# Decode attention on one core: K and V loaded as whole heads of 4 MB instead of halves of 2 MB

## The chip, the cores and the metric

The kernel runs on one core of a Trainium2 chip. The metric is the device time of one execution in microseconds (us). The kernel before takes 325.22 us (median; 324.94 to 325.31). The core's engines are named as in the profile: PE (TensorE matmul), PEld (weight load), DVE (VectorE), ACT (ScalarE), SP (SyncE, which issues the loads here). A trace's span, from its first to its last instruction, is about 2 us shorter than this time (322.9 us for the kernel before).

## The reference

One query row attends to 8,192 keys in each of 16 heads; all inputs are bfloat16.

```python
B, H, Sq, Sk, D = 1, 16, 1, 8192, 256      # q (1,16,1,256), k and v (1,16,8192,256)
scale  = D ** -0.5
scores = einsum("bhqd,bhkd->bhqk", q, k) * scale
p      = softmax(scores, axis=-1)
out    = einsum("bhqk,bhkd->bhqd", p, v)
```

K and V are 134.2 MB together and each byte is used once. A head has 4 MB of K and 4 MB of V.

## The kernel before

A head's 8,192 rows are laid over 128 partitions, 64 rows (columns of 256 elements) in each: 32 KB of a partition for a head. K and V come in halves of 32 columns: 2 MB, 16 KB in each partition. There are four slots of 2 MB for K and four for V.

```python
HALF = 32; K_SLOTS = V_SLOTS = 4; LAG = 4      # (cut: constants put on one line)
FIRST_CUT = (4, 4, 8, 16)                      # the first half of K0 in pieces
LAST_CUT, BEFORE_CUT = (16, 8, 4, 4), (16, 16) # the last two halves of V in pieces

kseq = [(h, x) for h in range(H) for x in range(2)]
for n, kx in enumerate(kseq):                  # order of loads: V four halves behind K
    items.append(("k", *kx))
    while nv <= n - LAG:
        items.append(("v", *kseq[nv])); nv += 1

# ... one load: waits until the half of four before it has been used
    if n >= slots:
        waits = [f"{kind}free{n - slots}"] + ([f"ktfree{n - slots}"] if kind == "k" else [])
    plan.op("sp", lambda e, ...: e.dma_start(b[:, at * D : (at + wd) * D], cols(t, h, c + at, c + at + wd)),
            f"{kind}{n}.{i}", waits, dma=(s, used[id(s)]))
```

For each half of K, DVE computes 24 columns of scores (a multiply with a sum, about 0.345 us a column) and PE the other 8 (16 transposes, a copy by ACT, 16 small matmuls). PE then multiplies the weights of an earlier head with its V ("P·V" below, 32 matmuls per half). One pass of PE's loop, a turn, is:

```python
for h in range(H):                  # PE's program, cut to its order
    softmax(h - 1); k_turn(2 * h); softmax2(h - 1); k_score(2 * h); lmm(h - 1)
    pv(2 * (h - 2))                 # first half of V of head h-2
    k_turn(2 * h + 1); k_score(2 * h + 1)
    pv(2 * (h - 2) + 1)             # second half
    final(h - 2)
```

## Time and profile before

A load is shared by 16 DMA engines. A row is the part of a load that goes to one partition, and moves as one packet. A landing record is the time at which one engine has finished its share. Loads are named by tensor and head: V13 (or v13) is V of head 13.

| view | reading |
|---|---|
| queue table | the loads take 98.1% of the span of the 16 DMA engines |
| busy times | DVE 86%, PE 69% of the span |
| packet records of the trace | 16 KB row: 611 ns (8 KB: 309, 4 KB: 159, 2 KB: 84, at the shortest 81), the most frequent value of each |
| landing records, mean of a load's 16 engines | one 2 MB load every 4.89 to 4.90 us |
| landing records, last engine | last piece of V at 319.65 us |
| PE timeline | last matmul ends at 320.86 us |

These are lines of the page of the kernel before: granted clock of PE, busy share of the DMA engines and GB/s, each in 40 equal slices of the span (9 is 90% or more), then the queue of the loads (packets, MB, share of the span) and the first line of the chain that ended last.

```profile
PEclk9999999999698998989595989777989697897799
DMA  7999999999999999999999999999999999999993
GB/s 276 421 436 428 421 430 428 424 426 426 431 428 426 428 428 428 432 426 424 432 426 434 426 424 430 428 428 429 426 430 426 430 427 428 428 426 428 426 417 120
q1 hardware_dynamic: 10224, 134.22, 98.1%
DVE 52%; DMA 37%; PE 5%; issue 5%; DVEq 1%; ACT 0%; SPq 0%
```

The chain names DVE most, because it follows each load back to the compute that freed its slot. The DMA line decides: no slice but the first and the last is below 9.

PE's timeline of the end of the kernel before (line 607 is P·V; the bracket is the idle time before the first instruction and what ended it):

```profile
299.91 8.81 PE L607 MATMUL acc<-Vb,E 128*1 128x256 bf16 x64 [1.33 <-DMA Vb<-in_v_dram]
308.56 0.38 PE L547 MATMUL misc<-ident,m 128*1 128x128 f32 x2
309.74 1.91 PE L607 MATMUL acc<-Vb,E 128*1 128x256 bf16 x16 [0.80 <-DMA Vb<-in_v_dram]
311.58 0.38 PE L558 MATMUL misc<-g,ones_row 1*128 1x1 f32 x2
311.89 1.91 PE L607 MATMUL acc<-Vb,E 128*1 128x256 bf16 x16
313.63 0.19 PE L587 MATMUL misc<-ones_col,lsum 128*1 128x1 f32 x2
313.69 7.17 PE L607 MATMUL acc<-Vb,E 128*1 128x256 bf16 x64
```

From the landing of the second half of V13 (299.87 us) PE has five blocks of 32 left and needs 20.9 us for them. It ends 1.2 us after the last load.

### The profile page before, as it was taken

To read this page: it belongs to the slowest core of one execution; us is meant where nothing else is said; L and a number is where in the kernel's file an instruction comes from. 1 tells how busy PE (TensorE), PEld (TensorE's weight loads), DVE (VectorE), ACT (ScalarE), POOL (GpSimd) and SP (SyncE) were. 2 spreads that over 40 slices of the span, in tenths; PEclk is the share of its full clock that TensorE was granted. 3 is DMA by queue.
4 is the path that set the end of the run, shared out by engine and by line. 5 is a ranking of instruction groups with operands and counts; after the bars stand their busy time and mean duration, and the time that the engine had idled before them with its cause. 6 is when DMAs were issued, how large, how long until landed. Compare 5 with 4: busy or idle time off the path is not lost.

```text
span 322.9 us, 6455 instructions
## 1 busy us (share of the span) xinstructions
PE 222.2 (69%) x2166; PEld 155.6 (48%) x2166; DVE 277.8 (86%) x1607; ACT 94.1 (29%) x185; POOL 0.2 (0%) x4
## 2 busy tenths in 40 slices
PE   1554328766586858686987756886665966668897
PEld 0333225655364635454564534564543644455565
DVE  3799999999999999999998988889988889888600
ACT  3362321432324242323142242212422123232010
POOL 0000000000000000000000000000000000000000
PEclk9999999999698998989595989777989697897799
DMA  7999999999999999999999999999999999999993
GB/s 276 421 436 428 421 430 428 424 426 426 431 428 426 428 428 428 432 426 424 432 426 434 426 424 430 428 428 429 426 430 426 430 427 428 428 426 428 426 417 120
DMA packets 10271, 134.37 MB, mean 416 GB/s; under 512 B 1154, under 2 KB 1171, under 8 KB 1940
## 3 DMA queue, kind: packets, MB, share of 16 engines
q1 hardware_dynamic: 10224, 134.22, 98.1%
q8 instruction: 5, 0.08, 0.1%
q14 instruction: 6, 0.05, 0.0%
q10 hardware_dynamic: 36, 0.02, 0.0%
HBM read 134.23 MB, written 0.01 MB: 416 GB/s over the span
## 4 chain that ended last, share of the span: by engine, by line
DVE 52%; DMA 37%; PE 5%; issue 5%; DVEq 1%; ACT 0%; SPq 0%
DVE prod L360 48%; DMA Kb<-in_k_dram 19%; DMA Vb<-in_v_dram 18%; PE acc L607 5%; DVE S L360 2%; DVE g L332 1%; DVE colf L286 0%; DVE recip L341 0%; DVEq L145 0%; DVE m L379 0%; ACT o L621 0%; DVEq L138 0%; DVEq L139 0%; SPq L319 0%; PE misc L558 0%
## 5 line engine op out<-in xcount | busy, mean ns | idle before, releaser
L360 DVE CUSTOM_DVE_ANT_0 prod<-Kb,qbc 128x256 bf16<-128x256 bf16 x768 | 269.1, 411 | 24.6 <-DMA Kb<-in_k_dram 15.7
L607 PE MATMUL acc<-Vb,E 128*1 128x256 bf16 x1024 | 147.4, 314 | 8.8 <-DMA Vb<-in_v_dram 8.8
L607 PEld LDWEIGHTS acc<-Vb,E 128*1 128x1 bf16 x1024 | 96.3, 96 | 52.4 <-DMA Vb<-in_v_dram 9.9
L502 ACT ACTIVATE KT<-tp 128x1024 bf16<-128x1024 bf16 x64 | 62.0, 1021 | 118.2 <-PE tp L493 118.2
L360 DVE DVE_READ_ACCUMULATOR2_ANT S<- 128x1 f32 x768 | 56.8, 74 | 0.0
L493 PE MATMUL tp<-identb,Kb 128*128 128x128 bf16 x512 | 38.2, 234 | 7.8 <-DMA Kb<-in_k_dram 7.8
L493 PEld LDWEIGHTS tp<-identb,Kb 128*128 128x128 bf16 x512 | 32.3, 105 | 15.7 <-issue 14.2
L519 PE MATMUL spe<-qcur,KT 128*128 128x1 bf16 x512 | 20.6, 165 | 19.7 <-ACT KT L502 19.7
L558 PE MATMUL misc<-g,ones_row 1*128 1x1 f32 x32 | 7.1, 287 | 36.1 <-DVE g L332 36.1
L519 PEld LDWEIGHTS spe<-qcur,KT 128*128 128x128 bf16 x512 | 16.4, 99 | 24.5 <-ACT KT L502 24.3
L621 ACT ACTIVATE o<-acc,recip 1x256 bf16<-1x256 f32 x16 | 7.4, 464 | 69.4 <-PE acc L607 69.4
L558 PEld LDWEIGHTS misc<-g,ones_row 1*128 1x128 f32 x32 | 5.7, 221 | 39.1 <-DVE g L332 38.8
L547 PE MATMUL misc<-ident,m 128*1 128x128 f32 x34 | 7.1, 293 | 18.6 <-DVE m L379 18.6
L547 PEld LDWEIGHTS misc<-ident,m 128*1 128x1 f32 x34 | 1.9, 82 | 22.0 <-DVE m L379 21.4
L565 ACT ACTIVATE negb<-misc 128x1 f32<-128x1 f32 x16 | 2.7, 171 | 27.4 <-PE misc L558 27.4
L332 DVE TENSOR_REDUCE g<-misc 1x1 f32<-1x128 f32 x17 | 4.7, 274 | 5.2 <-PE misc L547 5.2
L341 DVE RECIPROCAL recip<-misc 1x1 f32<-1x1 f32 x17 | 2.6, 151 | 4.6 <-PE misc L587 4.6
L572 ACT ACTIVATE E<-S,negb 128x64 bf16<-128x64 f32 x16 | 5.6, 348 | 0.7 <-ACT negb L565 0.2
L587 PE MATMUL misc<-ones_col,lsum 128*1 128x1 f32 x34 | 3.2, 164 | 3.7 <-ACT E L572 3.7
L439 ACT ACTIVATE qbc<-qb 128x256 bf16<-128x256 bf16 x14 | 5.6, 400 | 0.0
L532 ACT ACTIVATE S<-spe 128x16 f32<-128x16 f32 x16 | 2.9, 183 | 7.2 <-PE spe L519 7.2
L413 PE MATMUL tp<-q,identb 16*128 16x256 bf16 x15 | 4.1, 406 | 0.6 <-ACT qb L422 0.5
(29 smaller groups left out, 22.7 us busy)
## 6 DMA issues: line engine op xcount, KB each, us to landing
Kb<-in_k_dram SPq DMA_DIRECT2D x31, 2048.0 KB, 24.3
Vb<-in_v_dram SPq DMA_DIRECT2D x30, 2048.0 KB, 29.5
Vb<-in_v_dram SPq DMA_DIRECT2D x3, 1024.0 KB, 16.5
Kb<-in_k_dram SPq DMA_DIRECT2D x1, 1024.0 KB, 8.5
Kb<-in_k_dram SPq DMA_DIRECT2D x2, 256.0 KB, 3.0
Kb<-in_k_dram SPq DMA_DIRECT2D x1, 512.0 KB, 6.5
Vb<-in_v_dram SPq DMA_DIRECT2D x1, 512.0 KB, 12.7
Vb<-in_v_dram SPq DMA_DIRECT2D x2, 256.0 KB, 13.0
```

The costliest lines, as they stand in the source:

```text
L332: lambda e: e.tensor_reduce(g[0:1, s : s + 1], misc[s][0:1, MT0 : MT0 + P], AX.X, ALU.max),
L360: lambda e, slot=slot, c=c, col=col, h=h, r=(ttr - 1) % PROD: e.tensor_tensor_reduce(out=prod[:, r * D : (r + 1) * D], in0=Kb[slot][:, c * ...
L413: lambda e, i=i, src=src: e.matmul(bank[:, i * D : (i + 1) * D], lhsT=src[0], rhs=src[1], start=True, stop=True),
L439: lambda e: e.activation(out=qbc[:, s * D : (s + 1) * D], in_=qb[:, (h - 2) * D : (h - 1) * D], func=ACT.Copy),
L493: lambda e, c=c, hf=hf, i=(b * NH + hf) * P, view=view: e.transpose(view[:, i : i + P], Kb[slot][:, c * D + hf * P : c * D + (hf + 1) * P] ...
L502: lambda e, gn=gn, view=view: e.activation(out=KT[gn % KT_SLOTS][:, :], in_=view[:, 0 : GROUP * D], func=ACT.Copy),
L519: lambda e, b=b, hf=hf, oc=oc, gn=gn: e.matmul(spe[sl(h)][:, oc : oc + 1], lhsT=KT[gn % KT_SLOTS][:, (b * NH + hf) * P : (b * NH + hf + 1) ...
L547: lambda e: e.matmul(misc[s][0:1, MT0 : MT0 + P], lhsT=m[:, s : s + 1], rhs=ident[:, :], start=True, stop=True),
L558: lambda e: e.matmul(misc[s][:, BC0 : BC0 + 1], lhsT=ones_row[0:1, :], rhs=g[0:1, s : s + 1], start=True, stop=True),
L572: lambda e: e.activation(out=E[:, s * J : (s + 1) * J], in_=S[:, s * J : (s + 1) * J], func=ACT.Exp, bias=negb[:, h : h + 1], scale=SCALE, ...
L607: lambda e, c=c, col=col: e.matmul(a[0:1, 0:D], lhsT=E[:, col : col + 1], rhs=Vb[slot][:, c * D : (c + 1) * D], start=(x == 0 and c == 0), ...
L621: lambda e: e.activation(out=o[0:1, h * D : (h + 1) * D], in_=acc[s][0:1, 0:D], func=ACT.Copy, scale=recip[0:1, s : s + 1],),
```

## The change

Its intent: fewer and larger transfers, with rows of 32 KB instead of 16 KB, to come nearer to the peak of the DMA engines. K and V get two slots of 4 MB each instead of four of 2 MB; the SBUF used is the same. V runs one head behind K for the first eight heads, then two (before, four halves, which is two heads, throughout). Both halves of P·V move to the end of the turn, since V now lands whole.

```diff
-K_SLOTS = 2 * UNROLL
-V_SLOTS = 2 * UNROLL
-FIRST_CUT = (4, 4, 8, 16)
-LAST_CUT = (16, 8, 4, 4)
-BEFORE_CUT = (16, 16)
-LAG = 4
+K_CUTS = {0: (4, 4, 8, 16, 32)}
+V_CUTS = {14: (32, 16, 16), 15: (16, 16, 16, 8, 4, 4)}
+LAG_FROM = 8
@@ buffers
-        Kb = [sb([P, HALF * D], dt, "Kb") for _ in range(K_SLOTS)]
-        Vb = [sb([P, HALF * D], dt, "Vb") for _ in range(V_SLOTS)]
+        Kb = [sb([P, J * D], dt, "Kb") for _ in range(2)]          # J = 64 columns
+        Vb = [sb([P, J * D], dt, "Vb") for _ in range(2)]
@@ order of loads
+        for h in range(H):
+            loads.append(("k", h))
+            done = sum(kind == "v" for kind, _ in loads)
+            loads += [("v", x) for x in range(done, h + 1 - (1 if h < LAG_FROM else 2))]
@@ what a load waits for
-            if n >= slots:
-                waits = [f"{kind}free{n - slots}"] + ([f"ktfree{n - slots}"] if kind == "k" else [])
+            if h >= 2:
+                waits = [f"{f}{n}" for n in (2 * h - 4, 2 * h - 3) for f in ((kind + "free", "ktfree") if kind == "k" else ("vfree",))]
@@ PE's turn
                 lmm(h - 1)
                 if h + 1 < H:
                     q_row(h + 1)
-                if h >= 2:
-                    pv(2 * (h - 2))
...
             k_turn(2 * h + 1)
             k_score(2 * h + 1)
             if h >= 2:
+                pv(2 * (h - 2))
                 pv(2 * (h - 2) + 1)
                 final(h - 2)
```

More of the change, by code (lines that the diff above doesn't have):

```diff
@@ L213, in bass_standalone__mha_softmax__decode_kernel @@
         sems = {e: sem(f"s_{e}") for e in plan.ops}
-        s_k = [sem(f"s_k{i}") for i in range(K_SLOTS)]
-        s_v = [sem(f"s_v{i}") for i in range(V_SLOTS)]
-        s_first = [sem(f"s_f{i}") for i in range(len(FIRST_CUT) - 1)]
-        s_last = [sem(f"s_l{i}") for i in range(len(LAST_CUT) + len(BEFORE_CUT) - 2)]
+        s_k = [sem(f"s_k{i}") for i in range(2)]
+        s_v = [sem(f"s_v{i}") for i in range(2)]
+        s_piece = {}
         s_q = sem("s_q")
@@ L243, in bass_standalone__mha_softmax__decode_kernel, with cuts, pieces @@
         kseq = [(h, x) for h in range(H) for x in range(2)]
-        NIT = 2 * H
-        items, nv = [], 0
-        for n, kx in enumerate(kseq):
-            items.append(("k", *kx))
-            while nv <= n - LAG:
-                items.append(("v", *kseq[nv]))
-                nv += 1
-        items += [("v", *kx) for kx in kseq[nv:]]
-        n_of = {kx: n for n, kx in enumerate(kseq)}
-        def cuts(kind, n):
-            if kind == "k" and n == 0:
-                return FIRST_CUT
-            if kind == "v" and n == NIT - 1:
-                return LAST_CUT
-            if kind == "v" and n == NIT - 2:
-                return BEFORE_CUT
-            return (HALF,)
-        def landed(kind, n, c0, c1):
-            names, at = [], 0
-            if kind == "k" and n and n % K_SLOTS == 0:
-                names = [f"k{n}.0"] + [x for x in landed(kind, 0, c0, c1) if x != "k0.0"]
-                return names
-            for i, w in enumerate(cuts(kind, n)):
-                if at < c1 and at + w > c0:
-                    names.append(f"{kind}{n}.{i}")
-                at += w
-            return names
+        loads = []
+        for h in range(H):
+            loads.append(("k", h))
+            done = sum(kind == "v" for kind, _ in loads)
+            loads += [("v", x) for x in range(done, h + 1 - (1 if h < LAG_FROM else 2))]
+        loads += [("v", x) for x in range(sum(kind == "v" for kind, _ in loads), H)]
+        def cuts(kind, h):
+            return (K_CUTS if kind == "k" else V_CUTS).get(h, (J,))
+        def landed(kind, n, c0, c1):
+            h, x = kseq[n]
+            def pieces(h):
+                at = 0
+                for i, w in enumerate(cuts(kind, h)):
+                    if at < x * HALF + c1 and at + w > x * HALF + c0:
+                        yield i
+                    at += w
+            if kind == "k" and h and h % 2 == 0:
+                return [f"k{h}.0"] + [f"k0.{i}" for i in pieces(0) if i]
+            return [f"{kind}{h}.{i}" for i in pieces(h)]
         def dve(fn, name=None, waits=(), sem=None):
@@ L301, in bass_standalone__mha_softmax__decode_kernel @@
         plan.op("act", lambda e: e.dma_start(q16[:, :], q[0, :, 0, :]), "q", dma=(s_q, 16))
-        for kind, h, x in items:
-            n = n_of[(h, x)]
-            slots, sem_l, t, buf = (K_SLOTS, s_k, k, Kb) if kind == "k" else (V_SLOTS, s_v, v, Vb)
-            slot = n % slots
+        for kind, h in loads:
+            sem_l, t, buf = (s_k, k, Kb) if kind == "k" else (s_v, v, Vb)
             waits = []
-            if n >= slots:
-                waits = [f"{kind}free{n - slots}"] + ([f"ktfree{n - slots}"] if kind == "k" else [])
-            cs = cuts(kind, n)
+            if h >= 2:
+                waits = [f"{f}{n}" for n in (2 * h - 4, 2 * h - 3) for f in ((kind + "free", "ktfree") if kind == "k" else ("vfree",))]
+            cs = cuts(kind, h)
             at = 0
             for i, wd in enumerate(cs):
-                if kind == "k":
-                    s = sem_l[slot] if i == 0 else s_first[i - 1]
-                else:
-                    s = sem_l[slot] if i == len(cs) - 1 else s_last[i + (len(LAST_CUT) - 1) * (n == NIT - 2)]
+                s = sem_l[h % 2]
+                if i != (0 if kind == "k" else len(cs) - 1):
+                    s = s_piece[(kind, h, i)] = sem(f"s_{kind}{h}_{i}")
                 used[id(s)] = used.get(id(s), 0) + 16
@@ L318, in bass_standalone__mha_softmax__decode_kernel @@
                     "sp",
-                    lambda e, b=buf[slot], t=t, h=h, c=x * HALF, at=at, wd=wd: e.dma_start(
-                        b[:, at * D : (at + wd) * D], cols(t, h, c + at, c + at + wd)
+                    lambda e, b=buf[h % 2], t=t, h=h, at=at, wd=wd: e.dma_start(
+                        b[:, at * D : (at + wd) * D], cols(t, h, at, at + wd)
                     ),
-                    f"{kind}{n}.{i}",
+                    f"{kind}{h}.{i}",
                     waits,
@@ L349, in bass_standalone__mha_softmax__decode_kernel @@
         for n, (h, x) in enumerate(kseq):
-            slot = n % K_SLOTS
             if x == 0 and h % UNROLL == 0:
@@ L359, in bass_standalone__mha_softmax__decode_kernel @@
                 dve(
-                    lambda e, slot=slot, c=c, col=col, h=h, r=(ttr - 1) % PROD: e.tensor_tensor_reduce(
+                    lambda e, c=c, x=x, col=col, h=h, r=(ttr - 1) % PROD: e.tensor_tensor_reduce(
                         out=prod[:, r * D : (r + 1) * D],
-                        in0=Kb[slot][:, c * D : (c + 1) * D],
+                        in0=Kb[h % 2][:, (x * HALF + c) * D : (x * HALF + c + 1) * D],
                         in1=qbc[:, sl(h) * D : (sl(h) + 1) * D],
@@ L480, in k_turn @@
             h, x = kseq[n]
-            slot = n % K_SLOTS
             for gi in range(NG):
@@ L494, in k_turn @@
                                 view[:, i : i + P],
-                                Kb[slot][:, c * D + hf * P : c * D + (hf + 1) * P],
+                                Kb[h % 2][:, (x * HALF + c) * D + hf * P : (x * HALF + c) * D + (hf + 1) * P],
                                 identb[:, :],
@@ L600, in pv @@
             h, x = kseq[n]
-            slot = n % V_SLOTS
             a = acc[sl(h)]
@@ L609, in pv @@
                         lhsT=E[:, col : col + 1],
-                        rhs=Vb[slot][:, c * D : (c + 1) * D],
+                        rhs=Vb[h % 2][:, (x * HALF + c) * D : (x * HALF + c + 1) * D],
                         start=(x == 0 and c == 0),
```

## The prediction

> **What bounds it now.** The loads. The page's slice table shows DMA at 9 in every slice but the first and last, at about 428 GB/s; its queue table gives 98.1% of the 16 engines' span. DVE is busy 86%, PE 69%. In the trace's DMA packet records a 16 KB row takes 611 ns, and a 2 MB load (8 rows per engine, plus a 9 ns completion write) lands 4.90 us after the one before: no gaps. The last V piece lands at 319.65 us; the chain of waits ends with 64 back-to-back matmuls (7.04 us), which end near 320.9. PE and the loads finish almost together.
>
> **What the change does.**
> 1. Rows of 32 KB. Packets of 2, 4, 8 and 16 KB take 81, 159, 309 and 611 ns: about 604 ns per 16 KB plus 7 per packet. My estimate for 32 KB is 1,215 ns, against 1,222 for two. With half the completion writes that saves 0.065 us per 4 MB, over some 30 such loads 2.0 us (0.6%). The Trainium skill ("DMA: Bandwidth & Descriptors", "Why small descriptors are slow") also has a fixed cost per packet; here it is already about 1%, so little is left to take.
> 2. Slots of 4 MB: the same SBUF, freed in coarser steps. From DVE's 17.1 to 17.8 us per head, PE's durations and an estimated 9.73 us per load, K's next load can be issued with several us to spare; V, while it lags by one head (heads 2 to 7), with 0 to 4. v2, at about 64 us, is the tightest early.
> 3. A head's P·V now runs as one block of 64 matmuls at the end of a turn. V13 arrives whole at about 298 us (299.9 in the old order, less the saving). Before, 5 x 32 matmuls remained then; now 6 x 32 do. At 112 ns that is 21.5 us, plus about 0.8 us of softmax steps: 320.3 us at the earliest, later than the loads (about 317.7). The loads' gain is hidden behind PE.
> 4. PE is half idle before that block, so it starts slow. The clock records show 0.5 in windows of 3.41 us after little activity (300.8 to 304.2 us, for instance); P·V blocks of 32 took 3.65 us at full clock and 5.3 with such a window, as the skill says ("TensorE: Matmul & The Clock Gate", Part 1). One window costs about 1.7 us: the last matmul ends near 322.0. V15 also waits for V13's block to end (305 to 308.6 us, needed at about 307.8): a gap of 0 to 2 us in the queue.
>
> **On the critical path:** -2.0 us of packets, +1.5 us for PE's longer tail, +1.7 us of slow clock: about +1 us in sum.
>
> **Predicted: 326.2 us, range 323.6 to 329.0.** Chances: faster by over 2% 0.01, within 2% 0.96, slower by over 2% 0.03.
>
> **Right or wrong shows in:** 32 KB packets of about 1,215 ns and 431 GB/s in middle slices; K landings 19.5 us apart; DMA slices all 9, at most small dents; the last V landing at 317 to 319 us; P·V from V13 on back to back, PE ending 2 to 5 us after the last landing.
>
> **What would make it wrong:** full clock through the tail (then about 324.7); 32 KB rows no faster per byte (+2 us); repeated queue gaps from coarse V slots in heads 2 to 7, over 1 us each (+3 to +8 us); instruction fetches delayed by longer packets.

## More of the kernel before

SP issues the loads in program order: a load whose wait has not ended holds back all that follow.

Why there are no gaps shows in SP's timeline (start us, duration us, engine, line, operation, count), here of a little more than one head.

```profile
97.14 0.33 SPq L319 DMA_DIRECT2D Kb<-in_k_dram  x1
97.54 0.41 SPq L319 DMA_DIRECT2D Vb<-in_v_dram  x1
105.88 0.33 SPq L319 DMA_DIRECT2D Kb<-in_k_dram  x1
107.64 0.33 SPq L319 DMA_DIRECT2D Vb<-in_v_dram  x1
114.25 0.33 SPq L319 DMA_DIRECT2D Kb<-in_k_dram  x1
```

Loads are issued every 5 us on the average, in step with the freeing of halves. The V load issued at 107.64 lands, by the mean of its engines, at 131.43; the load ahead of it lands at 126.53, so it stood in the queue for 18.9 us before that. The queue never runs dry: after the first loads, none is issued less than 4.4 us before the mean landing of the load ahead.

## The result, and the profile after

The changed kernel takes 333.43 us (median of 5; 332.16 to 334.29). Its ratio to the kernel before is 1.0251, with a 95% interval of 1.0229 to 1.0273: slower by 2.5%. Here and below, a ratio is not quite the ratio of the medians that are quoted.

The lines of the page of the changed kernel that answer to those of before:

```profile
PEclk9999999957859588595876959595967878596799
DMA  7999999799998999999999899999999999999883
GB/s 249 438 435 433 426 435 435 283 423 431 433 412 352 435 415 415 443 380 411 431 435 439 332 435 443 439 435 431 411 435 443 439 428 427 423 431 419 344 356 153
q1 hardware_dynamic: 6192, 134.22, 95.8%
DMA 44%; DVE 29%; PE 20%; issue 4%; ACT 2%; SPq 0%; DVEq 0%
```

The rate in the good slices went up, from about 428 GB/s to about 432 (one 4 MB load every 9.71 us; single slices scatter around that). But there are holes: 283, 352, 380 and 332 GB/s in the slices at about 60, 103, 145 and 184 us, and two at the end. The clock line also has more low slices.

The holes, seen closely. Columns: stretch and its length in us; busy us (and instructions) of PE, PEld, DVE, ACT and POOL; PE's clock; DMA's busy share (which can come out a little over 1 in this view); GB/s. First the changed kernel, then the kernel before over the same stretches.

```profile
58.00:66.00 8.00, 6.35 (x65) 4.67 (x63) 5.80 (x35) 0.62 (x2) 0.00 (x0) 1.00 0.72 268
102.00:108.00 6.00, 3.81 (x40) 2.58 (x37) 3.71 (x24) 1.29 (x2) 0.00 (x0) 1.00 0.78 295
184.00:188.00 4.00, 2.99 (x35) 2.22 (x32) 3.97 (x24) 1.88 (x3) 0.00 (x0) 1.00 0.78 262
```

```profile
58.00:66.00 8.00, 5.51 (x66) 4.20 (x66) 7.96 (x48) 3.55 (x6) 0.00 (x0) 1.00 1.00 424
102.00:108.00 6.00, 5.82 (x43) 3.88 (x44) 6.00 (x37) 0.43 (x3) 0.00 (x0) 0.72 1.02 434
184.00:188.00 4.00, 2.93 (x31) 1.99 (x29) 2.81 (x16) 0.46 (x1) 0.00 (x0) 1.00 1.04 442
```

What SP waited for says which releases the loads now hang on (releaser, then us in total, times, longest; a long wait is not yet a hole, as the 185.2 us of the kernel before show). First the kernel before, then the changed one.

```profile
SPq L319 <- DVE S L360: 185.2, 28, 7.7
SPq L319 <- PE acc L607: 61.6, 19, 10.6
```

```profile
SPq L306 <- PE acc L591: 137.4, 11, 19.8
SPq L306 <- DVE S L346: 89.6, 9, 10.8
```

P·V was a minor releaser of loads before (line 607); now it is the main one (line 591), with waits of up to 19.8 us. The landing records of the trace give each late load. The steady spacing of 4 MB loads is 9.71 us, by the mean of the 16 engines' landings; what a load took beyond that is its gap:

| load | issued at | mean landing of the load ahead | issued ahead of it by | gap |
|---|---|---|---|---|
| v2 | 63.21 | 62.81 | -0.40 us | 2.73 us |
| v3 | 83.12 | 85.06 | 1.94 | 0.46 |
| v4 | 104.40 | 104.98 | 0.58 | 1.63 |
| v5 | 124.26 | 126.03 | 1.76 | 0.52 |
| v6 | 144.57 | 145.99 | 1.41 | 0.93 |
| k10 | 185.21 | 185.91 | 0.70 | 1.55 |
| v15, first piece | 314.66 | 313.91 | -0.74 | 2.72 |

The sum of the last two columns is nearly a constant: 2.2 to 2.4 us for the 4 MB loads and 2.0 us for the piece of V15. In these cases a load had to be issued that long before the mean landing of the load ahead of it, or time was lost. In the other runs the same sum is 2.1 to 3.7 us for loads of 2 and 4 MB, the most in front of k9 in the control below. The six gaps ahead of V14 sum to 7.8 us.

The packet records of the trace show what such a gap holds. V4's first packets start 0.95 us after the start of its issue (1.3 us on the mean over the engines); the engines had stood idle for 1.12 us on the mean, and 14 of the 16 first packets then took 1.39 to 2.09 us instead of 1.21, which is 0.57 us more per engine: 1.69 us in sum, against a gap of 1.63. In front of V3 and V5 the engines were idle for only 0.15 us, and most of the gap is slow first packets (0.43 and 0.37 us). Why these are slow is not shown.

One of these turns: SP's timeline, then four lines of PE's (five shorter ones cut; line 478 transposes of K, 591 P·V, 532 the first step of the next softmax).

```profile
104.40 0.33 SPq L306 DMA_DIRECT2D Vb<-in_v_dram  x1
104.77 0.43 SPq L306 DMA_DIRECT2D Kb<-in_k_dram  x1
```

```profile
87.22 1.05 PE L478 MATMUL tp<-identb,Kb 128*128 128x128 bf16 x16 [3.91 <-DMA Kb<-in_k_dram]
92.55 1.89 PE L478 MATMUL tp<-identb,Kb 128*128 128x128 bf16 x16
95.92 8.45 PE L591 MATMUL acc<-Vb,E 128*1 128x256 bf16 x64
104.40 0.38 PE L532 MATMUL misc<-ident,m 128*1 128x128 f32 x2
```

K4 lands on its last engine at 86.98 us and PE's turn starts. The P·V block of V2, whose data had been there since 77.25, starts 8.7 us later and ends at 104.37; only then is the slot of V2 free and V4 issued. But K5, the last load in the queue, has a mean landing of 104.98. V4's data start 1.63 us late, and K6, behind it in SP's order, with it.

At the end, PE's timeline shows the tail:

```profile
304.88 13.24 PE L591 MATMUL acc<-Vb,E 128*1 128x256 bf16 x96 [1.25 <-DMA Vb<-in_v_dram]
317.95 0.38 PE L532 MATMUL misc<-ident,m 128*1 128x128 f32 x2
318.17 1.91 PE L591 MATMUL acc<-Vb,E 128*1 128x256 bf16 x16
320.01 0.38 PE L543 MATMUL misc<-g,ones_row 1*128 1x1 f32 x2
320.32 1.91 PE L591 MATMUL acc<-Vb,E 128*1 128x256 bf16 x16
322.06 0.19 PE L572 MATMUL misc<-ones_col,lsum 128*1 128x1 f32 x2
322.12 7.15 PE L591 MATMUL acc<-Vb,E 128*1 128x256 bf16 x64
```

V13 lands (last engine) at 304.74 us and PE has six blocks of 32 left, which run without a pause to 329.27. The gap of 2.72 us in front of V15 lies in this stretch. It costs nothing further, because PE has not got there yet: the last V lands at 327.01, 2.3 us before the last matmul ends.

So the last matmul ends 8.4 us later than before (320.86). Of that, 5.0 us are the later start of the tail (299.91 to 304.88) and 3.4 us its greater length (20.9 to 24.4 us, for six blocks instead of five).

### The profile page after: what moved, and what is told of

Its sections match the earlier page's. It is cut to its first block, busy times and chain, and to the rows that moved or that the text cites. A ratio compares the mean times of both kernels' runs of the same rounds, so it can differ in the third digit from the quotient of the medians.

```text
span 331.3 us, 6400 instructions
## 1 busy us (share of the span) xinstructions
PE 228.8 (69%) x2166; PEld 166.2 (50%) x2166; DVE 277.4 (84%) x1607; ACT 94.1 (28%) x185; POOL 0.2 (0%) x4
## 4 chain that ended last, share of the span: by engine, by line
DMA 44%; DVE 29%; PE 20%; issue 4%; ACT 2%; SPq 0%; DVEq 0%
DVE prod L346 26%; DMA Kb<-in_k_dram 26%; PE acc L591 18%; DMA Vb<-in_v_dram 18%; ACT KT L487 2%; DVE S L346 1%; PE tp L478 1%; PE misc L543 1%; DVE g L319 0%; ACT E L557 0%; SPq L306 0%; DVE colf L276 0%; PE spe L504 0%; PE misc L572 0%; ACT negb L550 0%
## 5 line engine op out<-in xcount | busy, mean ns | idle before, releaser
L591 PE MATMUL acc<-Vb,E 128*1 128x256 bf16 x1024 | 141.4, 309 | 3.9 <-DMA Vb<-in_v_dram 3.9
L478 PE MATMUL tp<-identb,Kb 128*128 128x128 bf16 x512 | 48.5, 270 | 21.8 <-DMA Kb<-in_k_dram 21.8
L346 DVE DVE_READ_ACCUMULATOR2_ANT S<- 128x1 f32 x768 | 55.9, 73 | 0.0
L478 PEld LDWEIGHTS tp<-identb,Kb 128*128 128x128 bf16 x512 | 41.5, 124 | 27.5 <-issue 19.8
L543 PE MATMUL misc<-g,ones_row 1*128 1x1 f32 x32 | 8.0, 317 | 37.5 <-DVE g L319 37.5
L504 PE MATMUL spe<-qcur,KT 128*128 128x1 bf16 x512 | 21.4, 167 | 14.0 <-ACT KT L487 14.0
L504 PEld LDWEIGHTS spe<-qcur,KT 128*128 128x128 bf16 x512 | 17.3, 104 | 20.0 <-ACT KT L487 19.8
L543 PEld LDWEIGHTS misc<-g,ones_row 1*128 1x128 f32 x32 | 6.6, 257 | 40.5 <-DVE g L319 40.3
L408 ACT ACTIVATE qb<-tp 128x512 bf16<-128x512 f32 x7 | 3.9, 594 | 2.7 <-PE tp L399 2.7
```

The costliest lines, as they stand in the source:

```text
L346: lambda e, c=c, x=x, col=col, h=h, r=(ttr - 1) % PROD: e.tensor_tensor_reduce(out=prod[:, r * D : (r + 1) * D], in0=Kb[h % 2][:, (x * HAL ...
L408: lambda e: e.activation(out=qbc[:, a * D : b * D] if first else qb[:, (a - 2) * D : (b - 2) * D], in_=bank[:, 0 : (b - a) * D], func=ACT. ...
L478: lambda e, c=c, hf=hf, i=(b * NH + hf) * P, view=view: e.transpose(view[:, i : i + P], Kb[h % 2][:, (x * HALF + c) * D + hf * P : (x * HA ...
L504: lambda e, b=b, hf=hf, oc=oc, gn=gn: e.matmul(spe[sl(h)][:, oc : oc + 1], lhsT=KT[gn % KT_SLOTS][:, (b * NH + hf) * P : (b * NH + hf + 1) ...
L543: lambda e: e.matmul(misc[s][:, BC0 : BC0 + 1], lhsT=ones_row[0:1, :], rhs=g[0:1, s : s + 1], start=True, stop=True),
L591: lambda e, c=c, col=col: e.matmul(a[0:1, 0:D], lhsT=E[:, col : col + 1], rhs=Vb[h % 2][:, (x * HALF + c) * D : (x * HALF + c + 1) * D], s ...
```

## The experiments

Theory A: the queue runs dry because a slot of V is freed only when a whole head's P·V has ended, at the end of PE's turn, too late for the load that needs it next. Theory B: the 4 MB loads of 32 KB rows are slower themselves. Theory C: the slower clock of PE (0.82 of full speed in the profiled run, against 0.89 before) costs the time directly. The kernels were run in three groups; the kernel before ran beside each and took 324.9 us (medians 324.91 to 324.95). "Sum of gaps" is what all loads ahead of V14 took beyond the steady spacing of their size, from the profiled run: 0.9 us in the kernel before, 8.4 us in the changed one (7.8 of it in the six named loads). All runs gave correct results.

### V in halves, each issued when its own half is free

```diff
-V_CUTS = {14: (32, 16, 16), 15: (16, 16, 16, 8, 4, 4)}
+V_CUTS = {**{h: (32, 32) for h in range(14)}, 14: (32, 16, 16), 15: (16, 16, 16, 8, 4, 4)}
...
-                    waits,
+                    [f"vfree{2 * h - 4 + i}"] if kind == "v" and 2 <= h < H - 2 else waits,
```

(and a semaphore per slot for the first halves)

> The changed kernel with V of heads 0 to 13 loaded as two 2 MB pieces (16 KB rows), each issued when its own half of the slot is free; K, order and placement as changed. Theory A (the queue runs dry because a V load may be issued only when a whole 64-matmul block has ended): the first piece can be issued about 4.5 us earlier, which covers the lateness in front of v2 to v6 (2.7, 0.5, 1.6, 0.5 and 0.9 us by mean landings), so those 6.2 us go; the 1.55 us in front of k10 stays; the smaller rows give back about 0.9 us; P.V of head 13 can start a piece earlier, 1 to 2 us less at the end. Sum: about 326 to 328 us against 333.4. Theory B (the 4 MB transfers of 32 KB rows are themselves slower once the queue is busy): also faster, so this run alone does not tell them apart; with the next it does. Theory C (the slower PE clock, 0.82 against 0.89, costs the time by itself): little change, 332 to 334.

Measured: 326.88 us (325.79 to 327.82), ratio 1.0072 (1.0052 to 1.0092). The sum of gaps fell from 8.4 to 3.1 us; 0.53 us are left in front of v2 and 0.59 in front of v3, nothing over 0.3 us in front of v4 to v6. A gap of 1.10 us stood in front of k9. SP's timeline, at the place shown above, and the same stretch in the table of windows:

```profile
98.70 3.82 SPq L310 DMA_DIRECT2D Vb<-in_v_dram  x2
102.56 0.44 SPq L310 DMA_DIRECT2D Kb<-in_k_dram  x1
```

```profile
102.00:108.00 6.00, 1.56 (x20) 0.98 (x18) 3.44 (x20) 2.40 (x3) 0.00 (x0) 0.91 0.96 412
```

The first half of V4 now leaves at 98.70 us, 4.3 us before K5's mean landing of 102.96. PE's clock did not recover (0.83), so theory C does not explain the gain.

### The control: the same halves, but both wait for the whole slot

The edit is that of the run before without its last line.

> The same two 2 MB pieces of V with 16 KB rows as the run before it, but both pieces wait until the whole slot is free. Theory A: the gaps in front of v2 to v6 stay as in the changed kernel (about 6.2 us together), the smaller rows cost 0.9 us, the tail gains 1 to 2 us: about 332 to 333.5 us. Theory B (rows and transfer size): V's part of the loss goes, as in the run before it: 326 to 329 us. Theory C: 332 to 334.

Measured: 334.12 us (332.27 to 334.81), ratio 1.0274 (1.0236 to 1.0313). The sum of gaps is 9.3 us: v2 2.70, v3 0.98, v4 0.77, v5 0.96, v6 0.53, k9 1.74, k10 1.04. The two kernels load the same pieces in the same order with the same rows, and differ only in what a piece of V waits for: 7.2 us. Theory B fails: small rows and small transfers did not help. Both halves of V4 now leave together, as in the changed kernel:

```profile
104.58 0.80 SPq L310 DMA_DIRECT2D Vb<-in_v_dram  x2
105.43 0.43 SPq L310 DMA_DIRECT2D Kb<-in_k_dram  x1
```

Theory A's expectation held but for 0.6 us. The tail got shorter, as it had said (22.7 us from V13's last landing to the last matmul, against 24.5), but a gap at k9 came on top.

### V two heads behind K from head 3 on

```diff
-LAG_FROM = 8
+LAG_FROM = 3
```

> The changed kernel with one constant different: V lags K by two heads from head 3 on instead of from head 8 on. All rows, slots, placement and waits are unchanged. Theory A: v3 to v6 and k10 no longer come late (5.1 us of gaps go); the early gap of 2.7 us moves to k4, which waits for DVE to end K2, about 3 us. Sum about -4.5 us: 328 to 330 us. Theory B: no change, 333. Theory C: no change, 332 to 334.

Measured: 327.56 us (327.12 to 328.59), ratio 1.0079 (1.0062 to 1.0096), so 0.4 us better than expected. All rows are of 32 KB and all slots whole. One gap is left, in front of k4 (2.44 us); the sum of gaps is 3.0 us. With V two heads behind, a V load stands behind two others when its slot comes free (issued 12 to 19 us before the mean landing of the load ahead, from V3 on), and the late end of P·V no longer matters. The change of one constant took back 5.9 us. Coarse slots alone therefore make less than 3 of the 8 us: the rest takes coarse slots together with a lag of one head, which the change had shortened from two. The k10 gap went as well; it came from the switch of the lag at head 8, which puts K8 and K9 in a row. Only K9 and V7 are then in the queue while DVE works on K8: DVE needs it from 168.24 to 185.18 us, K10 is issued at 185.21, and V7's mean landing is at 185.91.

### P·V of the first half back in the middle of the turn

```diff
                 if h + 1 < H:
                     q_row(h + 1)
+                if h >= 2:
+                    pv(2 * (h - 2))
...
             if h >= 2:
-                pv(2 * (h - 2))
                 pv(2 * (h - 2) + 1)
```

> The changed kernel with the placement of P.V undone: the first half of a head's P.V stands between the two groups of transposes of a turn again, as before. Rows, whole slots, waits and order of loads as changed. Theory A (the whole slot is freed only by the end of the second half): the end of the second half moves little, 0 to 2 us earlier, so gaps in front of v2 to v6 shrink by at most 3 us together, and the end of the kernel gets up to 3 us longer because the last transposes now wait behind V13: 331 to 335. A rival (the one-block placement itself is the cause, by its slower clock): back to 326 or less.

Measured: 336.14 us (335.68 to 336.90), ratio 1.0331 (1.0308 to 1.0355), 1.1 us above the upper end of the expectation. The gaps of v2 to v6 stayed (2.42, 0.52, 1.40, 0.34 and 1.70 us; 6.4 together, against 6.3) and k10's grew to 2.86. From V13 on, PE needs 27.0 us instead of 24.4, because the last transposes now stand behind V13's first block. So the new placement is no cause of the loss; with whole V loads it is the better one.

### Idle matmuls to keep PE's clock up: three tries

The first try put 12 matmuls of 128x256, into an unused part of a PSUM bank, after each turn and 12 into PE's wait after the first transposes.

```diff
             k_turn(2 * h)
+            if h >= 2:
+                warm(h, 12)
...
                 final(h - 2)
+                warm(h, 12)
```

> The changed kernel with 24 idle matmuls (128x256, into an unused part of a PSUM bank) per head in PE's two waits, to keep its clock up; outputs unchanged. Theory C (clock): if the clock stays near 1.0, P.V blocks of 64 go from 8.5-9.9 to about 7.2 us and the time falls by all of the loss but the early gap, to about 326. Theory A: the clock only decides how late the blocks end: 1.5 us earlier each takes 0.5, 1.5, 0.5 and 0.9 us from the gaps at v3 to v6, leaves v2 and k10 with 1 to 1.5 us each, and shortens the tail by 1 to 2 us: 327 to 330. If the idle matmuls fail to lift the clock, neither is tested.

Measured: 334.33 us (332.94 to 334.80), ratio 1.0278 (1.0250 to 1.0305). Inconclusive: the mean clock rose to 0.88, but most P·V blocks still took 8.6 to 9.9 us, because the slow stretches fell into them.

The second try: 22 after each turn, 20 after the first transposes, 4 between the second transposes and their scores.

> The first try with idle matmuls did not lift the clock in the P.V blocks (still 8.6 to 9.9 us). Here 46 per head instead of 24, to fill nearly all of PE's waits. If the clock now stays at 1.0 and P.V blocks of 64 take about 7.2 us: theory A expects gaps of 0.5 to 1 us less at each late V load than in the changed kernel and a tail 1 to 2 us shorter, 327 to 331; theory C (the clock is the whole loss) expects 325 to 326. If P.V blocks stay above 8.5 us, the idle matmuls only delay PE: 334 to 337, and the clock's share stays open.

Measured: 332.63 us (330.01 to 334.35), ratio 1.0234 (1.0183 to 1.0285). The clock held, as the page's line of this run shows:

```profile
PEclk9999999999799999999999999999979979997999
```

P·V blocks took 7.15 us in most heads, and the sum of gaps fell to 4.0 us: v2 1.20, v4 0.86, k9 0.99, the others under 0.3. The time fell by less than a microsecond all the same (by the medians; the four runs lie at 330.0 to 331.2 and at 334.1 to 334.4, and the verdict on record is "unclear"). In the profiled run, 331.16 us, V13 landed 3.4 us earlier, but the tail was 1.5 us longer: the 22 idle matmuls behind V13's P·V take 2.6 us of it. The median is outside both expectations; the gaps are where theory A had them.

The third try moved those 22 from the end of a turn to the start of the next.

> The changed kernel with the 46 idle matmuls per head of the second try, which did hold the clock (0.98, P.V blocks 7.15 us), but those after the last P.V block of a turn moved to the start of the next turn, so that none stands in the tail. Theory A: the gaps in front of the late loads sum to about half of the changed kernel's (3.6 us in the second try against 7.8), and the tail is 1 to 2 us shorter than the changed kernel's: 327.5 to 330. Theory C (the clock is the whole loss): 325 to 326.

Measured: 331.12 us (328.30 to 332.44), ratio 1.0157 (1.0120 to 1.0195), clock 0.97. Its profiled run, the slowest of the four, has gaps of 4.37 us in front of v2 and 2.01 in front of v4: in the first turn, before the clock is up, the 22 idle matmuls took 4.54 us and held P·V of V0 back (it starts at 57.66 us instead of 54.51). V2's P·V block still took 9.65 us, in front of the gap at v4. The sum of gaps is 7.5 us, hardly less than the 8.4 of the changed kernel, but the gaps at v3, v5, v6 and k10 are gone, as in the second try. So this too missed theory A's range, by 1.1 us. Theory C fails as the whole cause: with the clock at 0.97 to 0.98 the kernel is still 1.6 to 2.3% slower than before. The second try's gaps speak for the clock deciding part of the lateness, the third's sum does not; its share of the time stays open, because the idle matmuls cost PE time of their own.

### Whole heads of K, halves of V

A version made from the findings: K loads as in the changed kernel; V in halves that wait for their own half; P·V placed as before the change; V lags K by one head at first, by one and a half to K8, then by two.

```diff
+            upto = 2 * h if h < 2 else 2 * h - 1 if h < LAG_FROM else 2 * h - 2      # LAG_FROM = 9
+            while nv < upto:
+                loads.append(("v", nv))      # nv counts halves of V
+                nv += 1
...
+                if kind == "v" and h >= 2:
+                    waits = [f"vfree{n - 4}"]
```

> A version made from the finding: K in whole heads of 32 KB rows as changed; V in halves of 2 MB that are issued when their own half is free; P.V placed as before; V lags K by one head for K2 at first, by one and a half up to K8, by two from K9 on. Theory A: no gap over 0.3 us in front of any load (none of the waits ends less than 2.3 us before the mean landing of the load ahead), the last V piece lands at 318 to 319 us instead of 319.65, the last matmul ends about 1 us after it: 323.5 to 325 us, ratio to the kernel before 0.995 to 1.0. If whole-head K loads lose time by themselves (their size, or K slots freed late), gaps appear in front of K loads and it stays at 327 or more.

Measured: 325.40 us (324.87 to 326.31), ratio 1.0013 (0.9995 to 1.0032), 0.4 us above the expectation. There is no gap over 0.3 us; the line of the page is whole again:

```profile
DMA  7999999999999999999999999999999999999992
q1 hardware_dynamic: 8208, 134.22, 97.7%
```

The last V lands at 318.51 us, as expected. But the last matmul ends at 320.79, 2.3 us later instead of 1: PE is the last to end, and the gain of the loads does not show in the time. K in whole heads costs nothing by itself.

### The same with 16 KB rows for K

Each K head but the first is loaded by two 2 MB transfers that both wait for the whole slot.

```diff
+                if kind == "k" and h:
+                    # a first transfer of columns 0 to 31 on the same semaphore (cut)
+                    at, wd = HALF, HALF
```

> The same as the run before it, but every K head but the first is loaded by two 2 MB transfers with 16 KB rows, both waiting for the whole slot. What the 32 KB rows of K are worth by themselves: 15 heads x 0.065 us = 1.0 us slower than the run before it by theory A; by theory B (large rows or transfers cost time) it is faster than it.

Measured: 326.40 us (325.63 to 327.35), ratio 1.0034 (1.0013 to 1.0055), in the same group as the run before it: 1.0 us slower. The intervals of the two ratios overlap a little, but the traces agree: from the landing of K0's last piece to that of V13 (mean landings) it takes 284.46 us, against 283.42. That is what the 32 KB rows of K, with the transfer in one piece, are worth, as expected. Theory B's sign is wrong.

### Whole heads of K, halves of V, with idle matmuls

The idle matmuls of the third try, in the version with halves of V.

> The version with whole heads of K and halves of V (325.4 us, no gaps, last V piece at 318.5, last matmul at 320.8 us) with the same idle matmuls at the start of turns. If its remaining 2.3 us between the last landing and the last matmul are PE's slow clock behind V13, they fall to about 1 us: 323.5 to 324.5 us, ratio 0.995 to 0.998. If the idle matmuls delay PE's steps instead, 325 to 327.

Measured: 324.78 us (324.02 to 325.27), ratio 0.9987 (0.9974 to 1.0001): the same as the kernel before, and 0.3 us above the expectation. In its profiled run PE now waits for the last pieces of V (0.16, 0.48 and 0.57 us), so the loads are last again; the slowest DMA engine landed its last piece at 319.82 us, against a mean of 317.64. No version tried here is faster than the kernel before by more than the noise.

## Why the prediction was wrong

It gave 326.2 us, 323.6 to 329.0, and put 0.96 on a result within 2%. Measured: 333.43 us, 2.5% slower.

- **What bounds the kernel: right.** The loads fill 98.1% of the engines' span, and only runs that left no large gap in them came back to 325 or 326 us.
- **The gain of the rows: right.** Expected 1,215 ns for a 32 KB packet and 2.0 us in all; the packets took 1,213 ns (median) and the spacing is 9.71 us against 9.79 for two loads of before: 0.08 us per 4 MB, about 2.2 us over 28 pairs up to V13. Undoing it for K alone cost 1.0 us. The Trainium skill ("DMA: Bandwidth & Descriptors", "Why small descriptors are slow") has a fixed cost per packet; here it is about 7 ns on 611.
- **The tail: right in itself.** Predicted: six blocks from V13's landing on, 24 us, PE ending 2 to 5 us after the loads. Measured: 24.4 us, 2.3 us after. The slow clock cost more than the 1.7 us allowed for it: half clock until 310.25 us made the first 96 matmuls take 13.24 us, where 112 ns each would give 10.75, 2.5 us less. The other 96 with the softmax steps took 11.15 us, 0.4 over 112 ns each, where 0.8 was allowed, so the sum fits in part by luck. The tail only started at 304.9 us instead of 298.
- **The step that failed** is this one of point 2: "V, while it lags by one head (heads 2 to 7), with 0 to 4" us to spare, with a gap near zero in the sum on the critical path. Measured: v2 to v6 had -0.4 to 1.9 us of lead where 2.2 to 2.4 were needed, and lost 6.3 us; the switch of the lag lost 1.55 us at k10, for which the same point had given K "several us to spare" (measured lead: 0.70). The 7.8 us of gaps less about 2.2 us of packets, plus 0.5 us at the start (K0's second half landed that much later; over all runs it lands at 13.5 to 14.3 us), give the 6.1 us by which V13's mean landing moved (297.96 to 304.06). The last list of the prediction named this case ("repeated queue gaps ... over 1 us each, +3 to +8 us"), but gave it too little weight, and the range ended below it.
- **Why it was mis-sized.** The lead that a load needs was taken too small. What I had allowed is known from my own working alone; the prediction's text does not hold it. (1) An issued load was taken to flow after some 1.3 us. The packet records bear that out for the first packets (1.2 to 1.3 us on the mean at v2, v4 and k10), but 0.4 to 0.5 us pass between an engine's last packet and its landing record, and the slow first packets add 0.6 to 0.8: together about the 2.2 to 2.4 us found at all six late 4 MB loads. (2) The queue was taken to run dry when the last engine of the load ahead lands. The bulk of the engines is done up to 2.3 us earlier (K3: mean 62.81, last 65.15), and PE's turn, which frees the slot, starts from the last one. Both errors have the same sign, 1.5 to 3.4 us in sum at the six loads. P·V blocks of 64 took 8.4 to 9.3 us in these heads, which by the same working had been allowed for; PE's slow stretches became longer, 6.8 to 10.2 us of half clock per head, against 3.4 to 6.8 before.
- **The clock.** The Trainium skill ("TensorE: Matmul & The Clock Gate", Part 1) gives two states, half and full, and a window of 3.4 us; the trace agrees (0.5 and 1.0 only, changing at multiples of 3.41 us). With the clock held up, the gaps halved in one run (4.0 against 8.4 us) and fell little in another (7.5), whose idle matmuls held back an early block. That it belongs to the cause, by making each block end later, is therefore argued; its share of the time stays open.

What is shown and what is argued: that the whole-slot wait of V makes the gaps is shown by the pair of runs that differ in that wait alone (334.12 and 326.88 us); that the short lag is needed for it is shown by the one-constant run (327.56); that K's whole loads are harmless is shown by the version with halves of V (325.40). That PE's longer tail costs time by itself is read from timelines; no run took it away alone. Instruction fetches, the last item of the prediction's list, had no run of their own; waiting for nothing that the profile shows ("issue") is 4% of the chain after and 5% before.

## What to carry to other kernels

When a kernel is bound by its loads, price a larger transfer by what its slot does to the issue times, not by its rate: find for each load the instruction that frees its slot, and ask that this ends 2.2 to 2.4 us (up to 3.7 in some runs here) before the mean landing of the load ahead of it in the queue. The same SBUF in fewer, larger slots frees later, and two of them per stream leave little lead; if whole slots are wanted, let the load that frees late stand further back in the order. At 98% of the engines' span there were 2 us to gain and 8 to lose.

## What the Trainium skill lacked or had wrong

- "DMA: Bandwidth & Descriptors" gives about 0.6 us to the first byte for loads issued from SP, and a fixed cost of 2.0 us for loads issued from GpSimd. The traces agree with the 0.6: the first packets of v2, v4 and k10 start 0.62 to 0.63 us after the end of the instruction that issues them. What the page lacks for this path is the whole cost of an issue that comes late: 2.2 to 2.4 us from the issue to the point from which a 4 MB load takes its 9.71 us to its mean landing (2.0 us for a 1 MB piece), of which the first packets' 1.4 to 2.1 us instead of 1.21 (V4) are a part.
- The same page's rule is at least 1 MiB per transfer; it says nothing of the slots that large transfers need. Here 2 MB loads ran at 428 GB/s and 4 MB loads at 432 (4,194,304 bytes in 9.79 and 9.71 us), and the kernel with the larger ones was 8 us slower, for want of free slots in time.
- The same page has no measured time for single large rows: 8, 16 and 32 KB packets took 309, 611 and 1,213 ns.
- No page gives a time for how far apart the 16 engines of one load finish: here 1.9 us or a little more between mean and last landing nearly throughout the kernel before, and 0.3 to 2.4 us in the changed one, smaller after the largest gaps (v2, v4, k10, v15).
- "TensorE: Matmul & The Clock Gate" has the clock fall after an idle window. Here it also fell after windows of 3.41 us in which PE was not idle: 36% busy from 287.18 to 290.59 us in the kernel before, 45% from 297.42 to 300.83. In the changed kernel it stayed low for up to three windows (10.24 us). 24 idle matmuls per head did not keep the clock up in most P·V blocks; 46 mostly did.
